# Second norm's scaling and power chain on GpSimd, small statistics first, urgent value and norm products allowed into dense work

## The chip, the cores and the metric

The kernel runs on one core of one Trainium2 chip. The metric is the device time in microseconds (us), as the median of several executions; a lower time is better. Beside the timed executions, each kernel has one profiled execution, whose trace gives what each engine did and when. The span of a profiled execution, from the first to the last instruction, is up to five us off the timed median. Engines in the trace: PE is TensorE's products (PEld its weight loads), DVE is VectorE, ACT is ScalarE, POOL is GpSimd, SP issues transfers.

## The reference, cut to what matters

Two pairs of layers on a sequence of 2048 tokens of width 512. Each A layer is attention with 32 heads that share one key and one value head of width 16; each B layer is two norms, a mixing MLP with shifted channels and an MLP of width 1792. Cut:

```python
def _A_ref(x, wq, wk, wv, wo):
    q = ...                                   # 32 heads of width 16
    k, v = x @ wk, x @ wv                     # one head, shared
    p = softmax(einsum("bhqd,bkd->bhqk", q, k) * 16 ** -0.5)
    return einsum("bhqk,bkd->bhqd", p, v)... @ wo

def _B_ref(x, w1, w2, w3, w4):
    h = gelu(layernorm(x) @ w1)               # then four channel groups shifted by 1, -1, 2, -2
    x1 = x + hs                               # hs = shifted @ w2
    return x1 + gelu(layernorm(x1) @ w3) @ w4

x = x + A(layernorm(x)); x = x + B(layernorm(x))      # layer 1
x = x + A(layernorm(x)); x = x + B(layernorm(x))      # layer 2
```

Note that B norms a row that was normed just before it: B receives layernorm(x), and norms that again. The kernel computes the second factor from the first variance by a chain of small operations, and this is the "second norm" of the title.

## The kernel before

The kernel is a Python program that plans before it emits. It declares operations with their reads, writes and an assumed duration, lets a planner place them on the five engines in simulated time, and then writes each engine's instructions in the planned order. On the chip each engine runs its list in that order and waits on semaphores. So the order is fixed, but the times are not: an instruction whose inputs come late holds up everything behind it in its engine's list.

Attention in one unit: TensorE makes scores (QK), ScalarE takes the exponential of 128x1024 of them into one of seven EA buffers, TensorE multiplies them by V (the "value product", accumulating in one PSUM bank). Some units are given to VectorE and GpSimd instead, as a "pair": VectorE turns scores into integers J (two instructions of 128x512), GpSimd, or VectorE if GpSimd is behind, adds constants (two instructions JK), and the bits read as bf16 are near the exponential. Dense work (projections and MLPs) and norms fill the gaps. When nothing is ready, TensorE multiplies zeros by ones ("filler"). This is meant to keep its clock up; a4 below shows a stretch in which it did not.

The parts that the change and the argument touch:

```python
# planner, choosing TensorE's next operation (cut)
stick = eng == "PE" and not dense and not joins and self.STICK is not None \
    and t < self.pe_end + 0.05 and self.pe_kind == "P"
...
key = (low.get(o, o.prio), o.seq)                 # smaller goes first; scores have 0, value products 2
...
if stick and o.prio > 2 and o.pe[0] == self.pe_kind and not any(... for x in due):
    key = (self.STICK, o.seq)                     # -1: a run of dense products is kept together

# when a pair may be declared (cut)
def attach(self, q):
    if sum(1 for t, b in self.pl.pool if t + 0.06 <= self.pl.now) >= self.FREE:   # FREE = 2 of 3 banks
        self.assign(self.pl.now, 1 - q.pe[3][0] // 2)     # also: pairs under way, VectorE's backlog

# rstd: the power -1/2 of the variance (and of the second norm's variance), cut
op("DVE", ... tensor_scalar(out=var, in0=mv, scalar1=EPS, op0=add))
if both:
    op("DVE", ... reciprocal(aux, var)); op("DVE", ... aux * mv); op("DVE", ... aux + EPS)
op("POOL", ... tensor_tensor(out=SM[:, 0:k], in0=SM[:, 2:2 + k], in1=MH, op=pow))   # one call for both

# mixer_in: the second norm's scaling
op("DVE", ... tensor_scalar(out=ZR[:, tb % 4], in0=Y[:, tb % 6], scalar1=SM[:, 1, tb], op0=mult), dur=0.265)

# ln_in: the next layer's normed rows also go to ZR
self.apply(self.ZR[:, tb % 4, :], src(tb), tb, ...)

URGE = ((10, 10, 10, 1.0), (10, 10, 10, 1.5, 10))     # base priority of what follows each chunk
```

The softmax here doesn't subtract the row's maximum and nothing guards it: scores larger than these inputs give would overflow.

## Time and profile before

| | before |
|---|---|
| timed median | 1616.96 us (1616.88 to 1617.77, 3 runs) |
| span of the profiled execution | 1615.1 us |
| exponentials on ScalarE | 1504, 1390.6 us |
| pairs on VectorE and GpSimd | 544 (1088 J instructions / 2) |
| fillers on TensorE | 1984 |
| end of the last exponential | 1549.26 us |

The lines are in the prediction below. The way to read them is to ask, for each stretch, which engine has no idle time: ScalarE in the two long attention stretches, none at the change of layers (760 to 935 us), TensorE and chains of waits in the tail after the last exponential.

Up to the end of its last exponential, ScalarE's time is the exponentials, the idle time ahead of them (66.6 us by the page), and the rest (Gelu, table loads, their waits): 1549.26 = 1390.6 + 66.6 + 92.1. After it comes the tail, 1615.1 - 1549.26 = 65.8 us.

### The profile page before, as it was taken

The page shows a single profiled execution, that of the slowest core. Times are in us where ns is not written, and L with a number is a line of the kernel's source. Part 1 is how long each engine was busy: PE and PEld are TensorE (multiplying, and loading weights), DVE is VectorE, ACT ScalarE, POOL GpSimd, SP SyncE. Part 2 cuts the span into 40 slices and gives each one's busy share as a digit, 9 for nine tenths or more (in the row PEclk, how much of TensorE's full clock was granted, in tenths as well). Part 3 has the DMA queues.
Part 4 walks back from the last instruction along what each step waited for, and adds up shares of the span by engine and source line. Part 5 has one row for each costly group of instructions (what it writes and reads, how often), then busy time and mean ns, then how long its engine had stood idle before and what let it go on. Part 6 is the DMA issues. An engine that isn't in the chain of part 4 may idle for free.

```text
span 1615.1 us, 63788 instructions
## 1 busy us (share of the span) xinstructions
PE 1567.6 (97%) x28953; PEld 654.9 (41%) x28953; DVE 1245.5 (77%) x2222; ACT 1500.5 (93%) x1580; POOL 1118.4 (69%) x1083
## 2 busy tenths in 40 slices
PE   8999999999999999999999999999999999999999
PEld 3333333434333333333333434333343334544555
DVE  8777887778887679887776678878678885778863
ACT  4999999999999999999998499999999998999952
POOL 4798877866787766776673477677777867768631
PEclk9999999999999999999999999999999999999999
DMA  6100010001000001000000000100000000000000
GB/s 207 17 6 5 7 18 6 6 4 17 7 6 4 6 4 19 6 4 2 2 2 2 3 9 9 19 4 5 9 18 5 6 5 15 16 8 7 6 17 19
DMA packets 32144, 21.55 MB, mean 13 GB/s; under 512 B 12672, under 2 KB 31360, under 8 KB 31872
## 3 DMA queue, kind: packets, MB, share of 16 engines
q1 hardware_dynamic: 31872, 17.47, 4.5%
q8 instruction: 226, 3.70, 1.0%
q14 instruction: 46, 0.38, 0.1%
HBM read 7.90 MB, written 2.10 MB: 6 GB/s over the span
## 4 chain that ended last, share of the span: by engine, by line
ACT 64%; PE 33%; DVE 2%; issue 0%; DMA 0%; POOL 0%; SPq 0%; POOLq 0%
ACT EA L994 59%; PE PB L612 12%; PE PB L950 10%; PE PB L1073 8%; ACT G L1403 2%; PE PB L769 1%; ACT L994 1%; ACT GP L1323 1%; ACT L1403 1%; ACT L1323 0%; DVE ZR L752 0%; DVE ST L723 0%; DMA X<-in_A_x_dram 0%; DVE J L1015 0%; PE PB L878 0%
## 5 line engine op out<-in xcount | busy, mean ns | idle before, releaser
L994 ACT ACTIVATE EA<-PB 128x1024 bf16<-128x1024 f32 x1504 | 1390.6, 1105 | 66.6 <-PE PB L1073 33.8
L1025 POOL TENSOR_SCALAR JK<-J 128x1024 uint16<-128x1024 uint16 x983 | 1035.6, 1054 | 402.4 <-DVE J L1015 257.4
L1015 DVE TENSOR_SCALAR J<-PB 128x512 uint16<-128x512 f32 x1088 | 702.4, 683 | 185.1 <-PE PB L950 181.1
L950 PE MATMUL PB<-QT,KT 32*128 32x512 bf16 (+1 forms) x4608 | 624.4, 359 | 30.5 <-ACT EA L994 18.6
L1073 PE MATMUL PB<-EA,VP 128*32 128x256 bf16 (+1 forms) x6784 | 388.4, 265 | 0.5
L950 PEld LDWEIGHTS PB<-QT,KT 32*128 32x128 bf16 x4608 | 161.3, 91 | 448.0 <-ACT EA L994 351.4
L1073 PE MATMUL PB<-JK,VD 128*32 128x256 bf16 (+1 forms) x4864 | 291.3, 265 | 2.9 <-POOL JK L1025 1.9
L1073 PEld LDWEIGHTS PB<-EA,VP 128*32 128x32 bf16 x6784 | 157.1, 95 | 175.3 <-issue 149.6
L612 PE MATMUL PB<-ONES,NIL 128*32 128x512 bf16 x1984 | 177.1, 387 | 7.4 <-DVE ZR L752 2.8
L1073 PEld LDWEIGHTS PB<-JK,VD 128*32 128x32 bf16 x4864 | 114.9, 95 | 128.0 <-issue 78.8
L612 PE MATMUL PB<-ZT,W 128*32 128x512 bf16 (+2 forms) x2816 | 166.6, 341 | 0.0
L1073 PE MATMUL PB<-J,VD 128*32 128x256 bf16 (+1 forms) x2432 | 154.9, 264 | 1.3 <-DVE J L1015 0.8
L612 PE MATMUL PB<-W,G 128*32 128x512 bf16 x1792 | 122.9, 380 | 0.3 <-DVE X L1279 0.3
L1396 DVE CAST G<-PB 128x512 bf16<-128x512 f32 (+2 forms) x126 | 72.3, 582 | 34.7 <-PE PB L612 33.4
L612 PEld LDWEIGHTS PB<-ZT,W 128*32 128x32 bf16 x2816 | 67.7, 96 | 26.1 <-issue 13.0
L1025 DVE TENSOR_SCALAR JK<-J 128x1024 uint16<-128x1024 uint16 x105 | 73.2, 702 | 2.9 <-PE PB L1073 1.9
L1073 PEld LDWEIGHTS PB<-J,VD 128*32 128x32 bf16 x2432 | 60.6, 95 | 35.4 <-issue 21.6
L612 PEld LDWEIGHTS PB<-ONES,NIL 128*32 128x32 bf16 x1984 | 49.6, 96 | 42.4 <-issue 11.2
L745 POOL TENSOR_TENSOR SM<-SM,MH 128x4 f32<-128x4 f32 (+4 forms) x30 | 31.7, 1058 | 40.8 <-DVE SM L737 24.8
L1133 DVE TENSOR_TENSOR OS<-ACCF,PB 128x512 bf16<-128x512 bf16 (+1 forms) x72 | 44.6, 622 | 17.7 <-PE PB L1127 17.3
L612 PEld LDWEIGHTS PB<-W,G 128*32 128x32 bf16 x1792 | 42.2, 96 | 31.8 <-issue 11.7
L1403 ACT ACTIVATE G<-G 128x3584 bf16<-128x3584 bf16 (+2 forms) x18 | 46.0, 2601 | 9.4 <-DVE G L1396 9.3
(88 smaller groups left out, 861.5 us busy)
## 6 DMA issues: line engine op xcount, KB each, us to landing
OT<-OS SPq DMA_DIRECT2D x424, 8.0 KB, 1.8
W<-in_B_w_dram SPq DMA_DIRECT2D x2, 1792.0 KB, 14.4
QT<-QS SPq DMA_DIRECT2D x40, 64.0 KB, 2.4
X<-in_A_x_dram SPq DMA_DIRECT2D x8, 256.0 KB, 5.4
out_dram<-OUTB SPq DMA_DIRECT2D x16, 128.0 KB, 1.7
OT<-OS SPq DMA_DIRECT2D x104, 4.0 KB, 1.7
W<-in_B_w_dram SPq DMA_DIRECT2D x2, 512.0 KB, 8.4
WQ<-in_A_wq_dram SPq DMA_DIRECT2D x1, 512.0 KB, 5.0
```

Of the source, the lines that this page charges most:

```text
L612: ins = e.matmul(self.PB[32 * g:32 * g + 32, bank, 0:n], lhsT=lhsT[:, 32 * g:32 * g + 32], rhs=rhs, start=start, stop=stop, tile_position= ...
L745: op("POOL", lambda e: e.tensor_tensor(out=self.SM[:, 0:k, a:b], in0=self.SM[:, 2:2 + k, a:b], in1=self.MH[:, 0:k, a:b], op=ALU.pow), read ...
L769: ins = e.transpose(self.PBH[:, L.bank, j * 512 + i * 128:j * 512 + (i + 1) * 128], self.ZR[:, tb % 4, dc * 128:(dc + 1) * 128], self.IDENT)
L950: ins = e.matmul(self.PB[:, bank, j * n:(j + 1) * n], lhsT=self.KT[32 * h:32 * h + 32, la, (kb + j) * 128:(kb + j + 1) * 128], rhs=self.QT ...
L994: o = q.feeds = op("ACT", lambda e: e.activation(self.EA[:, ea, :, :], self.PB[:, b0:b0 + 2, :], ACTF.Exp, scale=0.25), writes=bk + [("EA" ...
L1015: o = op("DVE", lambda e, i=i, L=L: e.tensor_scalar(out=J[:, i * 512:(i + 1) * 512], in0=self.PB[:, L.bank, :], scalar1=128 * LOG2E * 0.25 ...
L1025: x = op(eng, lambda e, k=k, r=r: e.tensor_scalar(out=self.JK[:, r, :], in0=J, scalar1=float(self.STEPS[k]), scalar2=1.0, op0=ALU.add, op1 ...
L1073: ins = e.matmul(self.PB[32 * x:32 * x + 32, self.ACC, p * hw:p * hw + hw], lhsT=v[:, la, kb + j, :], rhs=ap[:, i, j * w + u * hw:j * w + ...
L1133: op("DVE", lambda e: e.tensor_tensor(out=self.OS[:, m, 0:n], in0=acc, in1=self.PB[:, M.bank, 0:n], op=ALU.mult), reads=[("ACCF", m)], wri ...
L1323: return e.activation(self.GP[:, par, :, 2:2 + n], self.GP[:, par, :, 2:2 + n], ACTF.Gelu_apprx_tanh)
L1396: op("DVE", lambda e, f=f, L=L: e.tensor_copy(self.G2[:, f, 0:n], self.PB[:, L.bank, 0:n]), writes=[L, ("G2", f)], dur=t_ps(n), give=L)
L1403: ins = e.activation(self.G2[:, a:a + 7, 0:n], self.G2[:, a:a + 7, 0:n], ACTF.Gelu_apprx_tanh)
```

## The change

It takes 32 scalings and the small norm instructions off VectorE, and changes the planner's rules. The intent: VectorE is relieved for pairs; small statistics go first; value products that ScalarE is about to wait for are "pinned" ahead of dense work; urgent norm work breaks a run of dense products; the last chunk's work gets a high priority and a buffer of its own; the next layer's normed rows get the buffer QS, so that they need not wait for ZR. Cut to its core:

```diff
+    PINNED = -2
+    RUSHED = 1.2
@@ planner
         stick = ... and self.pe_kind == "P" \
+            and not any((0 < o.prio <= self.RUSHED if o.side else self.closing) and o.ready <= t + 1e-9 for o in h)
+        pinned = {p for u in self.units[-3:] if not u.placed for p in u.preds
+                  if p.eng == "PE" and p.prio == 2 and not p.placed} if eng == "PE" and not dense else ()
+            if eng == "ACT" and self.closing and o.side and not all(u.placed for u in self.units[-4:]):
+                continue
+            if o in pinned:
+                key = (self.PINNED, o.seq)
@@ kernel
-    URGE = ((10, 10, 10, 1.0), (10, 10, 10, 1.5, 10))
+    URGE = ((10, 10, 10, 1.0), (10, 10, 10, 1.5, 1.0))
+    RUSH = ((10, 10, 10, 1.0), (10, 10, 10, 5, 1.0))     # priority of a block's norm products, 5 before
@@ rstd: a power call for each norm, the small instructions on POOL (not in the head)
-            op("DVE", ... reciprocal(aux, var)) ...
+            op(eng, ... tensor_tensor(out=aux, in0=one, in1=one, op=mult)) ...
@@ ln_in
+        base = (self.QS, "QS") if la else (self.ZR, "ZR")
@@ mixer_in
-            op("DVE", lambda e, tb=tb: e.tensor_scalar(
+            op("POOL", lambda e, tb=tb: e.tensor_scalar(
...
-               dur=0.265, port=True)
+               dur=0.71, prio=self.QUICK, port=True)
@@ last MLP: Gelu output in the EA buffers
-                op("ACT", lambda e, f=f, L=L: e.activation(self.G2[:, f, 0:n], ...
+                op("ACT", lambda e, f=f, L=L: e.activation(self.G2E[:, f, 0:n], ...
```

## The prediction

> **What bounds the kernel now.** I read the page first, then the busy time of the engines in four stretches that I chose from the 40 slices, then what ScalarE waits for, then ScalarE and TensorE in order of time at its gaps. All figures below are of the one profiled execution of the kernel before (span 1615.1 us; the timed median is 1616.96 us).
>
> The page's engine row and its three costliest rows; columns of a row: line, engine, operation, output and input, count, then busy us and mean ns, then idle time before it:
>
> ```profile
> PE 1567.6 (97%) x28953; PEld 654.9 (41%) x28953; DVE 1245.5 (77%) x2222; ACT 1500.5 (93%) x1580; POOL 1118.4 (69%) x1083
> ...
> L994 ACT ACTIVATE EA<-PB 128x1024 bf16<-128x1024 f32 x1504 | 1390.6, 1105 | 66.6 <-PE PB L1073 33.8
> L1025 POOL TENSOR_SCALAR JK<-J 128x1024 uint16<-128x1024 uint16 x983 | 1035.6, 1054 | 402.4 <-DVE J L1015 257.4
> L1015 DVE TENSOR_SCALAR J<-PB 128x512 uint16<-128x512 f32 x1088 | 702.4, 683 | 185.1 <-PE PB L950 181.1
> ...
> L612 PE MATMUL PB<-ONES,NIL 128*32 128x512 bf16 x1984 | 177.1, 387 | 7.4 <-DVE ZR L752 2.8
> ```
>
> PE's 97% is not a bound everywhere: the last row is products of zeros that only keep TensorE busy. Four side by side are one step of 512 columns; 112 equal products in the tail take 6.05 us, so a step is 6.05/28 = 0.216 us and the 1984/4 = 496 filler steps are 107 us of room. The exponentials are done in two ways: 1504 on ScalarE (1390.6/1504 = 0.925 us each), and 1088/2 = 544 "pairs" by a bit trick on VectorE and GpSimd.
>
> The stretches (columns: PE, PEld, DVE, ACT, POOL busy us and count, granted clock, DMA share, GB/s):
>
> ```profile
> 40.00:760.00 720.00, 701.63 (x11972) 276.17 (x11964) 579.52 (x979) 718.39 (x760) 552.90 (x528) 1.00 0.04 8
> 760.00:935.00 175.00, 168.64 (x2864) 69.35 (x2866) 124.12 (x242) 142.37 (x145) 90.20 (x88) 1.00 0.01 2
> 935.00:1550.00 615.00, 602.00 (x12341) 260.11 (x12338) 481.24 (x852) 603.12 (x637) 452.66 (x435) 1.00 0.04 9
> 1550.00:1615.10 65.10, 60.25 (x1288) 34.17 (x1286) 25.99 (x62) 18.51 (x23) 5.53 (x6) 1.00 0.06 21
> ```
>
> In the first and third ScalarE is full (718 of 720, 603 of 615): there only fewer exponentials on ScalarE, or no gaps, shorten the time. The second is the change of layers: 175 - 142.4 = 32.6 us of ScalarE are lost. The fourth is the tail, 65 us with no exponential, bound by TensorE and by chains.
>
> ScalarE's gaps in order of time (start, length, what, and in brackets the idle time before it and who ended it):
>
> ```profile
> 879.15 9.27 ACT L994 ACTIVATE EA<-PB 128x1024 bf16<-128x1024 f32 x10
> 898.57 1.02 ACT L994 ACTIVATE EA<-PB 128x1024 bf16<-128x1024 f32 x1 [10.15 <-PE PB L1073]
> ...
> 930.66 34.94 ACT L994 ACTIVATE EA<-PB 128x1024 bf16<-128x1024 f32 x38 [8.38 <-PE PB L950]
> ...
> 1181.93 18.44 ACT L994 ACTIVATE EA<-PB 128x1024 bf16<-128x1024 f32 x20 [3.11 <-PE PB L1073]
> ...
> 1369.39 1.94 ACT L994 ACTIVATE EA<-PB 128x1024 bf16<-128x1024 f32 x2 [5.19 <-PE PB L1073]
> ```
>
> The releaser L1073 is a value product (exponentials times V). The exponentials rotate through seven EA buffers; ScalarE stops when the product that reads the oldest has not run. TensorE was busy with dense work instead:
>
> ```profile
> 1365.16 3.19 PE L612 MATMUL PB<-W,G 128*32 128x512 bf16 x56
> 1368.18 1.05 PE L612 MATMUL PB<-YT,WQ 128*32 128x256 bf16 x32
> 1369.05 0.40 PE L1073 MATMUL PB<-EA,VP 128*32 128x128 bf16 x16
> ```
>
> **What the Trainium skill says.** "GPSIMD Engine Reference", section Engine selection, calls one-input elementwise work on GpSimd roughly line-rate and two-input work about twice as slow. The trace agrees on the first: 1024 elements in a median of 1044 ns; on two inputs, X<-Y,X takes 1169 ns for 512, about double per element. "Advanced Engine Details and Errata", VectorE Performance Modes, Mode Summary, says that GpSimd and VectorE's two-port modes block each other at a shared port. The trace fits: the scaling ZR<-Y,SM of VectorE takes 256 ns at best and 1134 at worst, and the add of epsilon on four numbers 149 to 1028, the excess being about one GpSimd add. "Perfetto Trace Analysis", Identifying the Most-Contended Engine, warns that matmul busy share is no measure of headroom; here the fillers are why.
>
> **The change, part by part.**
>
> 1. VectorE to GpSimd. Off VectorE go 32 scalings ZR<-Y,SM (16.8 us busy), the reciprocal, product and add of the two-norm groups (1.5 + 3.9 + 3.8), and 26 of the 30 epsilon adds (9.5 x 26/30 = 8.2): 34.2 us. GpSimd gets 32 x about 0.6 (half of a 1024-element add plus the reading of a scalar: 19 us), 26 + 27 small ones at about 0.2 (as its 8-element copies, 191 to 219 ns: 10.6 us) and power as two calls of 4 numbers, 2 x 1.015 against 1.641 for 8 (0.4 x 7 groups: 2.7 us): about 32 us on an engine that idles 497. VectorE spends 702.4/544 = 1.29 us per pair plus 73.2/544 = 0.13 for the adds that fall back on it, 1.43. So at most 34.2/1.43 = 24 more pairs, each worth 0.925 us of ScalarE: 22 us. A pair is declared only while two PSUM banks are free and few pairs are under way, and VectorE already idles 185 us waiting for score products, so I take a third: 8 pairs, **-8 us**. TensorE pays for a pair 3.5 steps (two score steps, three half steps of values) against 1.5: 2 x 0.216 = 0.43 us, 3.5 us for 8, from 81 us of fillers in these stretches.
>
> 2. Value products pinned ahead of dense work. In the full stretches the waits of this kind sum to 9.5 us (0.2 + 3.1 at 1176-1182, 5.2 + 0.4 + 0.4 + 0.2 at 1364-1382). Nearly all should go: **-8 us**. At the change of layers some 20 us of such waits go too, but there it is no gain by itself: ScalarE runs out of scores whose keys exist (the 8.38 us wait for L950 at 930), and the keys come when TensorE has done the dense chain. Fed without gaps, ScalarE reaches that wait earlier and waits longer. Only a shorter chain (transposes and norm products no longer behind a run of dense products; QS in place of ZR for the next layer's rows) helps: **-2 us**.
>
> 3. The tail. From the output projection at 1553.88 to the last product at 1612.1 are 58.2 us. The dense products in it, counted in steps: 8 (WO) + 126 (W,G) + 36 (288 of 256 columns) + 12 (W,GP) + 42 (224 of 384) = 224 x 0.216 = 48.4 us. So 9.8 us are chain waits, fillers and transposes:
>
> ```profile
> 1580.67 0.67 PE L612 MATMUL PB<-ONES,NIL 128*32 128x512 bf16 x8
> 1581.54 1.02 PE L612 MATMUL PB<-ONES,NIL 128*32 128x512 bf16 x12 [0.20 <-DVE ST L723]
> 1582.75 1.26 PE L612 MATMUL PB<-ONES,NIL 128*32 128x512 bf16 x20 [0.18 <-DVE MV L725]
> 1584.66 0.40 PE L612 MATMUL PB<-ONES,NIL 128*32 128x512 bf16 x4 [0.65 <-DVE ZR L752]
> ```
>
> The last chunk's work now has priority 1.0 instead of 10, and its Gelu output goes into the free EA buffers, so it need not wait until older chunks' products have read G2. Its two norm chains then lie beside 24 us of older chunks' dense work (12 W,G, 6 of W3, 6 W,G). The waits of 1580.67-1587.3 (6.6 us less 0.8 of transposes) should be filled; the 1.8 us after the projection stay, since the Gelu of 1550.57-1556.84 still comes after the last exponential: **-6 us**. The longer power chain on GpSimd costs nothing there: scaling now ends at 1562.2; with 0.2 + 0.7 + 3 x 0.2 + 0.7 + 2 x 0.6 us after the statistics at 1558.1, plus hand-overs, it ends at much the same time.
>
> Sum: -8 - 8 - 2 - 6 = -24 us. The whole order of instructions is planned anew, and slots won in one place are partly lost in another; I keep nine tenths: -22 us, 1595 us.
>
> **Rivals.**
> - GpSimd becomes the wait. Scalings stand in its queue among 1.04 us adds and lengthen each norm chain by 2 to 3 us, and more adds fall back on VectorE (105 now). For it: the chains matter at the change of layers. Against: 31% idle, and a wait of at most 8.4 us for its inputs, not for itself. Alone it would take back the pairs' 8 us and add some 3: about 1606.
> - TensorE becomes the bound: removed gaps in ScalarE merely displace dense work, as at the change of layers, and the tail inherits it. For it: the stretch 1360-1400 has only 1.39 us of fillers. Against: 60 us of fillers in the third stretch as a whole. Then only the tail and a few pairs remain: about 1606.
> - VectorE's backlog was what held pairs back. For it: it is 80% busy in the first stretch, and the worst shared-port cases vanish with it. All 24 pairs would give -22 instead of -8, and the waits at the change of layers might shrink by 5 more: about 1577.
>
> **Range and chances.** The first two rivals put the upper side at about 1606 and a poor replanning at 1611; the third, taken half, puts the lower side at 1580. 2% below is 1584.6: it needs the third rival nearly whole, chance 0.15. Slower by 2% would need a broken chain; each part moves work to an engine with room: 0.01.
>
> **What would show it.** Fewer ScalarE exponentials and as many more J rows (8 halves: 1496 and 1104); the total of ScalarE waiting for L1073 from 33.8 us to under 10; a wait for L950 at the change of layers longer than 8.4 us; no filler group in the tail after the projection longer than 2 us; VectorE's rows for ZR<-Y,SM gone and about 0.6 us each on GpSimd. It would be wrong if the number of pairs fell, if the stretch between the layers shortened or lengthened by over 6 us, or if GpSimd's scaling took over 1 us.

## The result, and the profile after

The changed kernel took 1598.39 us (median of 4 runs, 1597.78 to 1599.63) against 1616.97 us of the kernel before on the same chip (1616.88 to 1617.77). The ratio is 0.9883 with a 95% interval of 0.9869 to 0.9897. Ratios are the mean time of one kernel's fast runs over that of the other's fast runs of the same rounds, so they are not quite the ratio of the medians quoted. The prediction was 1595 us with a range of 1580 to 1611.

The page of the changed kernel, engine row and the rows that answer to those of before (line, engine, operation, output and input, count, then busy us and mean ns, then idle before):

```profile
PE 1553.5 (97%) x28709; PEld 648.2 (41%) x28709; DVE 1214.7 (76%) x2145; ACT 1506.4 (94%) x1585; POOL 1133.5 (71%) x1149
...
L1017 ACT ACTIVATE EA<-PB 128x1024 bf16<-128x1024 f32 x1509 | 1397.6, 1088 | 47.1 <-PE PB L973 37.6
...
L1038 DVE TENSOR_SCALAR J<-PB 128x512 uint16<-128x512 f32 x1078 | 698.9, 683 | 195.1 <-PE PB L973 190.9
...
L625 PE MATMUL PB<-ONES,NIL 128*32 128x512 bf16 x1764 | 153.8, 388 | 6.6 <-DVE ZR L773 1.7
```

VectorE is busy 30.8 us less than before. But the relief bought no pairs: there are 1078/2 = 539, five fewer, and ScalarE has five exponentials more. What fell is ScalarE's idle time ahead of exponentials, from 66.6 to 47.1 us, and the number of fillers.

The same sum as before: the last exponential ends at 1536.75 us = 1397.6 + 47.1 + 92.05, and the tail is 1597.5 - 1536.75 = 60.75 us. So the span's 17.6 us less are:

| term | before | after | difference |
|---|---|---|---|
| exponentials on ScalarE | 1390.6 | 1397.6 | +7.0 |
| idle time ahead of them | 66.6 | 47.1 | -19.5 |
| rest of ScalarE up to there | 92.1 | 92.05 | 0 |
| tail | 65.8 | 60.75 | -5.1 |

Where the idle time went shows in ScalarE's timeline of the changed kernel (start, length, what; in brackets the idle time before it and who ended it):

```profile
871.64 16.85 ACT L1017 ACTIVATE EA<-PB 128x1024 bf16<-128x1024 f32 x18
894.73 12.26 ACT L1017 ACTIVATE EA<-PB 128x1024 bf16<-128x1024 f32 x13 [6.24 <-PE PB L1096]
...
927.62 124.49 ACT L1017 ACTIVATE EA<-PB 128x1024 bf16<-128x1024 f32 x135 [14.73 <-PE PB L973]
```

L1096 is the value product's line now, L973 that of the scores. At the change of layers the long wait for a value product is 6.2 us and not 10.2, and the wait for the scores of the last keys grew from 8.4 to 14.7 us, as ScalarE arrives there earlier; the scores come 3.0 us earlier than before (927.62 against 930.66). After it the kernel before had gaps of 11.0 us in sum (10.5 of them for value products, 0.5 for scores); the changed kernel shows none that the timeline lists.

TensorE in the tail, in order of time:

```profile
1550.63 1.48 PE L625 MATMUL PB<-W,G 128*32 128x512 bf16 x24
1551.94 1.92 PE L625 MATMUL PB<-ZT,W 128*32 128x256 bf16 x64
1553.68 1.47 PE L625 MATMUL PB<-W,G 128*32 128x512 bf16 x24
1554.98 2.76 PE L625 MATMUL PB<-W,GP 128*32 128x512 bf16 x48
1557.57 4.92 PE L625 MATMUL PB<-W,G 128*32 128x512 bf16 x88
```

The last chunk's products (ZT,W and W,GP) now lie inside the older chunk's W,G. In the kernel before, 224 of those ran ahead of them, 112 before the last chunk's transposes (IDENT,ZR) and 112 after:

```profile
1563.62 0.62 PE L769 MATMUL PB<-IDENT,ZR 128*128 128x128 bf16 x8
1564.17 6.23 PE L612 MATMUL PB<-W,G 128*32 128x512 bf16 x112
1570.22 3.01 PE L612 MATMUL PB<-ZT,W 128*32 128x256 bf16 x104
```

The fillers for the last norm, which took some five us in the kernel before, are one group of 0.79 us.

The operations that moved, on GpSimd:

```profile
L1314 POOL TENSOR_SCALAR ZR<-Y,SM 128x512 bf16<-128x512 bf16 x32 | 22.2, 711 | 0.9
...
L758 POOL TENSOR_SCALAR SM<-MV 128x4 f32<-128x4 f32 x12 | 2.8, 233 | 19.5 <-DVE MV L738 18.7
```

### The profile page after: what moved, and what is told of

The parts are those of the page before. It is cut to its first block, busy times and chain, and to the rows that moved or that the text cites. A ratio compares the mean times of both kernels' runs of the same rounds, so it can differ in the third digit from the quotient of the medians.

```text
span 1597.5 us, 63318 instructions
## 1 busy us (share of the span) xinstructions
PE 1553.5 (97%) x28709; PEld 648.2 (41%) x28709; DVE 1214.7 (76%) x2145; ACT 1506.4 (94%) x1585; POOL 1133.5 (71%) x1149
## 4 chain that ended last, share of the span: by engine, by line
ACT 73%; PE 24%; DVE 3%; DMA 0%; issue 0%; POOL 0%; SPq 0%; POOLq 0%
ACT EA L1017 68%; PE PB L625 9%; PE PB L973 7%; PE PB L1096 6%; ACT G L1428 2%; ACT L1017 1%; PE PB L791 1%; ACT GP L1348 1%; ACT L1428 1%; DVE ST L736 0%; ACT L1348 0%; DVE G L1421 0%; DMA X<-in_A_x_dram 0%; DVE J L1038 0%; PE PB L901 0%
## 5 line engine op out<-in xcount | busy, mean ns | idle before, releaser
L1017 ACT ACTIVATE EA<-PB 128x1024 bf16<-128x1024 f32 x1509 | 1397.6, 1088 | 47.1 <-PE PB L973 37.6
L1048 POOL TENSOR_SCALAR JK<-J 128x1024 uint16<-128x1024 uint16 x955 | 1009.3, 1057 | 354.6 <-DVE J L1038 229.6
L973 PE MATMUL PB<-QT,KT 32*128 32x512 bf16 (+1 forms) x4608 | 623.8, 360 | 26.0 <-ACT EA L1017 15.0
L1096 PE MATMUL PB<-EA,VP 128*32 128x256 bf16 (+1 forms) x6796 | 385.3, 264 | 0.9 <-DVE QT L1108 0.5
L973 PEld LDWEIGHTS PB<-QT,KT 32*128 32x128 bf16 x4608 | 160.5, 91 | 434.8 <-ACT EA L1017 312.9
L1096 PE MATMUL PB<-JK,VD 128*32 128x256 bf16 (+1 forms) x4840 | 288.7, 265 | 2.9 <-POOL JK L1048 1.9
L1096 PEld LDWEIGHTS PB<-EA,VP 128*32 128x32 bf16 x6796 | 159.0, 95 | 159.1 <-issue 128.7
L625 PE MATMUL PB<-ZT,W 128*32 128x512 bf16 (+2 forms) x2816 | 170.4, 342 | 0.2
L1096 PEld LDWEIGHTS PB<-JK,VD 128*32 128x32 bf16 x4840 | 114.3, 95 | 135.3 <-issue 83.3
L625 PE MATMUL PB<-ONES,NIL 128*32 128x512 bf16 x1764 | 153.8, 388 | 6.6 <-DVE ZR L773 1.7
L1096 PE MATMUL PB<-J,VD 128*32 128x256 bf16 (+1 forms) x2420 | 153.3, 263 | 1.4 <-DVE J L1038 0.6
L625 PE MATMUL PB<-W,G 128*32 128x512 bf16 x1624 | 114.4, 383 | 1.1 <-ACT G L1428 1.1
L1048 DVE TENSOR_SCALAR JK<-J 128x1024 uint16<-128x1024 uint16 x123 | 80.9, 664 | 4.9 <-PE PB L1096 3.6
L625 PEld LDWEIGHTS PB<-ZT,W 128*32 128x32 bf16 x2816 | 63.8, 96 | 32.4 <-issue 18.6
L1096 PEld LDWEIGHTS PB<-J,VD 128*32 128x32 bf16 x2420 | 59.8, 95 | 37.1 <-issue 22.7
L625 PEld LDWEIGHTS PB<-ONES,NIL 128*32 128x32 bf16 x1764 | 43.7, 96 | 42.1 <-issue 10.4
L1428 ACT ACTIVATE G<-G 128x3584 bf16<-128x3584 bf16 (+2 forms) x18 | 46.0, 2602 | 14.9 <-DVE G L1421 14.8
L1157 DVE TENSOR_TENSOR OS<-ACCF,PB 128x512 bf16<-128x512 bf16 (+1 forms) x72 | 44.8, 622 | 17.5 <-PE PB L1151 16.7
L756 POOL TENSOR_TENSOR SM<-SM,MH 128x4 f32<-128x4 f32 (+3 forms) x39 | 37.0, 950 | 22.3 <-DVE SM L758 19.4
L625 PEld LDWEIGHTS PB<-W,G 128*32 128x32 bf16 x1624 | 37.3, 96 | 29.7 <-issue 13.8
```

Of the source, the lines that this page charges most:

```text
L625: ins = e.matmul(self.PB[32 * g:32 * g + 32, bank, 0:n], lhsT=lhsT[:, 32 * g:32 * g + 32], rhs=rhs, start=start, stop=stop, tile_position= ...
L756: op("POOL", lambda e: e.tensor_tensor(out=out, in0=src, in1=self.MH[:, 0, a:b], op=ALU.pow), reads=tags + [("MH",)], writes=tg(r), dur=0. ...
L973: ins = e.matmul(self.PB[:, bank, j * n:(j + 1) * n], lhsT=self.KT[32 * h:32 * h + 32, la, (kb + j) * 128:(kb + j + 1) * 128], rhs=self.QT ...
L1017: o = q.feeds = op("ACT", lambda e: e.activation(self.EA[:, ea, :, :], self.PB[:, b0:b0 + 2, :], ACTF.Exp, scale=0.25), writes=bk + [("EA" ...
L1048: x = op(eng, lambda e, k=k, r=r: e.tensor_scalar(out=self.JK[:, r, :], in0=J, scalar1=float(self.STEPS[k]), scalar2=1.0, op0=ALU.add, op1 ...
L1096: ins = e.matmul(self.PB[32 * x:32 * x + 32, self.ACC, p * hw:p * hw + hw], lhsT=v[:, la, kb + j, :], rhs=ap[:, i, j * w + u * hw:j * w + ...
```

## The experiments

Twelve kernels ran, in three groups of four, each group on one chip with the kernel before. All gave a correct result. "Planned anew" means that the planner ran with the stated rules, so that every instruction may change place. "Held order" means that the plan of before or after was kept, and only the named instructions were moved. On the three chips the kernel before took 1616.99, 1617.56 and 1616.96 us (medians of seven runs each). Where a difference in us is taken between kernels of different groups, or to the 1616.97 us of before above, it can be off by the half microsecond by which these differ.

| run | kernel | median us | ratio to before, 95% interval |
|---|---|---|---|
| a1 | after, norm work to VectorE, held order | 1617.15 | 0.9979 to 1.0026 |
| a2 | before, norm work to GpSimd, held order | 1620.82 | 1.0010 to 1.0040 |
| a3 | before, late value products ahead, held order | 1618.62 | 0.9991 to 1.0021 |
| a4 | before, tail rules only | 1616.64 | 0.9977 to 1.0010 |
| b1 | before with the pin only, planned anew | 1627.51 | 1.0050 to 1.0080 |
| b2 | after without the pin, planned anew | 1643.65 | 1.0146 to 1.0176 |
| b3 | before, a neutral constant changed | 1625.35 | 1.0033 to 1.0063 |
| b4 | after, norm work on VectorE, planned anew | 1604.07 | 0.9902 to 0.9936 |
| c1 | before with pin and QS, planned anew | 1613.14 | 0.9959 to 0.9992 |
| c2 | after, pairs at one free bank | 1592.07 | 0.9833 to 0.9872 |
| c3 | after, the same neutral constant changed | 1616.31 | 0.9978 to 1.0008 |
| c4 | after, six planner constants changed | 1581.67 | 0.9768 to 0.9797 |

The first theory, A, was that of the prediction put sharply: the order of TensorE's work made the gain, and the engine of the norm work did not. Its rivals are named in the expectations.

### a1: the norm work back on VectorE, order held

```diff
             self.pl.run(self.pump)
+            for o in self.scalings:          # 32 scalings, 53 small norm instructions
+                self.pl.order[o.eng].remove(o)
+                o.eng = "DVE"
+                self.pl.order[o.eng].append(o)
+            self.pl.renumber()               # sort each engine's list by planned start
```

> The changed kernel with every instruction in its planned place, only that the 32 scalings and the 53 small norm instructions go back from GpSimd to VectorE (the second power stays a second call). Theory A (the order of TensorE's work made the gain, the engine of the norm work did not): 1596 to 1603 us, same within 0.3%. Rival B (relief of VectorE and of the shared port made it): 1606 us or more, with VectorE's busy time up by some 30 us and waits of ScalarE back.

Measured: 1617.15 us (1614.12 to 1622.19), the whole gain gone, and inside the range of rival B. The waits of ScalarE, first the changed kernel, then a1 (total us, times, longest):

```profile
ACT EA L1017 <- PE PB L973: 37.6, 11, 18.3
```

```profile
ACT EA L1031 <- PE PB L987: 47.5, 33, 18.4
```

There are 22 more short waits for scores, most of 0.2 to 0.7 us. The waits for value products stayed at 8.8 us, and the tail too (1612.2 - 1551.42 = 60.8 us). So theory A failed as stated: in this order the engine does matter. The likely reason is that VectorE's list had no room planned for these instructions; the extra hand-overs between VectorE and GpSimd in the power chain are another, which a1 doesn't separate. In the profile of a1 the granted clock also dips to 0.91 in three 20-us slices and not in one (540 to 560, which the changed kernel has as well), and ScalarE's gaps at 1414 to 1426 and 423 to 440 lie in the two others, about 3 us each. Whether the dips made these gaps or the gaps the dips is not known. They do not carry the whole loss: the two runs with a mean granted clock of 0.996 (0.998 to 0.999 in the changed kernel) still took 1614 us.

### a2: the norm work to GpSimd in the order of before

```diff
+            for o in self.scalings:          # 32 scalings, 26 epsilon adds
+                ... o.eng = "POOL" ...
```

> The kernel before with every instruction in its planned place, only that the 32 scalings and 26 epsilon adds run on GpSimd. Theory A: 1613 to 1620 us, no gain, and the gaps of ScalarE before the value products stay (33.8 us in total). Rival B: 1609 us or less.

Measured: 1620.82 us, just above what A expected, and clearly not rival B. VectorE's busy time fell from 1245.5 to 1226.6 us, the waits for value products stayed at 33.8 us, and nothing was gained. a1 and a2 together show a one-sided thing: in these fixed orders, work put on an engine cost at once, while work taken off it gave nothing back by itself, as the other instructions stay in their places.

### a3: late value products moved ahead, order held

```diff
+            for u in self.units:
+                for p in u.preds:
+                    if p.eng == "PE" and p.prio == 2:        # a value product
+                        t = (when its inputs were planned to be there)
+                        if p.start > t + 4.0:
+                            p.start = t + 4.0
+            self.pl.renumber()
```

> The kernel before, with the 63 value products that were planned over 4 us after their inputs moved forward to 4 us after them; nothing else changes place. Theory A: ScalarE's waits for value products after the change of layers fall from 10.3 us to under 3 and the time falls by 7 to 11 us, to 1606 to 1610; at the change of layers the waits for value products go too, but the wait for scores grows from 8.4 us to some 20, so nothing is gained there. Rival C (TensorE is the bound, and gaps only displace dense work): 1614 us or more.

Measured: 1618.62 us, no gain; rival C's time. In ScalarE's timeline of a3, at the place where before waited 5.19 us for a value product:

```profile
1366.83 1.94 ACT L1010 ACTIVATE EA<-PB 128x1024 bf16<-128x1024 f32 x2 [3.02 <-PE PB L1089]
1371.29 4.91 ACT L1010 ACTIVATE EA<-PB 128x1024 bf16<-128x1024 f32 x5 [2.53 <-PE PB L966]
```

L1089 is the value product, L966 the scores. The wait was not removed but handed on: two exponentials start earlier, and the next one waits for scores that still stand behind the dense run, since in the plan they were placed for the late time. Over the whole run waits for value products fell from 33.8 to 8.8 us, waits for scores rose from 31.8 to 45.0 and those of Gelu for VectorE from 9.3 to 19.9. Moving one of two things that stand behind a dense run gained nothing here.

### a4: the tail rules alone

```diff
-    URGE = ((10, 10, 10, 1.0), (10, 10, 10, 1.5, 10))
+    URGE = ((10, 10, 10, 1.0), (10, 10, 10, 1.5, 1.0))
 (and the last Gelu's output in EA, as in the change)
```

> The kernel before with only the last chunk's priority 1.0 in place of 10 and its Gelu output in the EA buffers; up to the last exponential the order is that of before. Theory A: last exponential at the same time, the tail after it shorter by 4 to 6 us: 1611 to 1613. Rival D (the tail also needs the breaking of dense runs): under 2 us gained, 1615 or more.

Measured: 1616.64 us, rival D's time. Two things are in it. In the profiled execution the last exponential ended at 1552.26 us, 3.0 later than before, although the order up to there is the same. The view of 20-us stretches of a4 (busy time and count of GpSimd, granted clock, DMA share, GB/s) has the reason:

```profile
880.00:900.00 20.00, 4.39 (x5) 0.83 0.01 2
```

Before had 1.00 there. This is a lapse of TensorE's clock, in which eight filler-sized products took 1.04 us in place of 0.61. The order of work there is that of before, so no moved instruction explains it. The tail itself became 1614.8 - 1552.26 = 62.5 us, 3.3 less than before and 1.8 more than after. Its timeline:

```profile
1566.50 0.62 PE L782 MATMUL PB<-IDENT,ZR 128*128 128x128 bf16 x8
1567.05 6.23 PE L624 MATMUL PB<-W,G 128*32 128x512 bf16 x112
1573.10 3.01 PE L624 MATMUL PB<-ZT,W 128*32 128x256 bf16 x104
```

The transposes broke in, but the last chunk's first products (ZT,W) still waited for 112 products of an older chunk, which the stick rule kept together. In the changed kernel they stand between 24 and 24. So the priority and the buffer are worth about 3 of the tail's 5 us in the profile. The breaking of the runs is the likely source of the rest, but it was not tested alone.

The median of the timed runs shows no gain, but each run lists its mean granted clock. Three of a4's four runs have a mean granted clock of 0.997, the profiled one among them, and took 1616.55 to 1616.88 us. The fourth has 0.999 and took 1614.65. The kernel before had 0.998 or 0.999 in all seven runs on this chip, and those with 0.999 average 1616.97. So at an equal clock the tail rules gain about 2.3 us, by one run. Why a4 had the lower clock in three runs of four stays open.

### b1 and b2: the pin alone, and everything but the pin

After the first four runs I formed theory E: the parts work through one joint plan, and the pin pays only together with others. Both kernels are planned anew.

```diff
 # b1: before, plus
+        pinned = {...}
+            if o in pinned:
+                key = (self.PINNED, o.seq)
 # b2: after, with
-                  if p.eng == "PE" and p.prio == 2 and not p.placed} if eng == "PE" and not dense else ()
+        pinned = ()
```

> The kernel before, planned anew with the pinned value products only. After the four runs with held order, the revised theory E: the gain is in the joint order, the pin takes away the waits after the keys of layer 2 but alone it makes those keys later. E: waits of ScalarE for value products after the keys under 2 us (before 10.3), the wait for the first scores of layer 2's last keys longer than 8.4 us and later than 930.7 us by 20 us or more, the time no better: 1617 to 1632. The prediction's step (pin worth 8 us by itself): 1606 to 1611.

> The changed kernel, planned anew without the pinned value products. E: most of the gain is lost or turned into a loss, since all the other parts move work of other kinds ahead of value products: 1620 to 1645, with waits of ScalarE for value products after the keys over 25 us in total. If the pin only displaced work (rival C): 1598 to 1606.

Measured: b1 1627.51 us, 10 us slower than before; b2 1643.65 us, 45 us slower than after. The lines of ScalarE, b1's timeline first, then b2's waits:

```profile
938.96 137.51 ACT L1008 ACTIVATE EA<-PB 128x1024 bf16<-128x1024 f32 x149 [13.06 <-PE PB L964]
```

```profile
ACT EA L1017 <- PE PB L1096: 62.1, 30, 7.6
```

In b1 the waits for value products after 945 us fell from 10.5 to 2.6 us (I had expected under 2), so the pin does what it is meant to. But the scores of the last keys came at 938.96 us, 8.3 us later than before (I had expected 20 or more), and ScalarE waited 13.06 us for them. Just before stands a wait that the kernel before did not have:

```profile
919.36 3.28 ACT L1419 ACTIVATE G<-G 128x1792 bf16<-128x1792 bf16 x2 [11.17 <-DVE G L1412]
```

By the sum used above, b1's idle time ahead of exponentials is 55.0 us, 11.6 less than before. The exponentials take 4.3 us more (1507 of them), and the rest and the tail together 17.4 us more, of which this wait before a Gelu is 11.2. So the pin shortened the waits that it aims at, and the time was lost at the change of layers. That the pin alone gains 8 us did not come out; but b1 is one plan, and b3 below shows that 10 us between two plans can be luck. b2 shows the other side: with all the other parts and no pin, ScalarE waits 62.1 us for value products, 36.0 of them after 945 us. These 45 us are more than twice the largest difference that b3 and c3 below put down to luck, so among the other parts of the change the pin is needed.

### b3 and c3: how much a plan is worth by luck

```diff
-    MARGIN = 0.15
+    MARGIN = 0.151          # b3 in before, c3 in after
```

The constant is a margin in the planner's arithmetic. It has no meaning for the work, it only decides which of nearly equal choices is taken, and from the first different choice on the order differs (and with it a few pairs: 542 in both b3 and c3, where before has 544 and after 539).

> The kernel before, with one constant of its planner (the margin that it adds before an instruction of TensorE) at 0.151 instead of 0.150 us, which changes no work, only the order that is planned. It measures how much a new plan is worth by luck. E: differs from before by 5 us or more, probably slower (1622 to 1635), since before was the best of its neighbours. Rival F (the plan is robust): within 2 us of 1617.

> The changed kernel with the margin constant 0.151 in place of 0.150, the counterpart of b3. E: the changed kernel was a lucky plan as well: 1608 to 1620, so that the change is worth some 10 to 17 us with this constant too (b3 is 1625.4). Rival F (the plan of the changed kernel is robust): within 3 us of 1598.4.

Measured: b3 1625.35 us, 8.4 us slower than before; c3 1616.31 us, 17.9 us slower than after. Both expectations held, rival F fell in both. In c3 the waits for value products are 26.0 us (8.8 in after), in b3 40.4 us (33.8 in before). With this constant the same change is worth 1625.35 - 1616.31 = 9.0 us and not 18.6. ScalarE's exponentials, b3 first, then c3:

```profile
L994 ACT ACTIVATE EA<-PB 128x1024 bf16<-128x1024 f32 x1506 | 1393.4, 1102 | 73.8 <-PE PB L1073 40.4
```

```profile
L1017 ACT ACTIVATE EA<-PB 128x1024 bf16<-128x1024 f32 x1506 | 1396.3, 1089 | 63.3 <-PE PB L973 36.0
```

The same sum for both constants tells what the two comparisons have in common. The rest and the tail are taken together, since in b3 one Gelu more stands ahead of the last exponential.

| what the change does to | constant 0.150 (before, after) | constant 0.151 (b3, c3) |
|---|---|---|
| exponentials on ScalarE | +7.0 | +2.9 |
| idle time ahead of them | -19.5 | -10.5 |
| rest of ScalarE and tail | -5.1 | -1.5 |
| span | -17.6 | -9.1 |

In both, most of the gain is idle time ahead of exponentials, and no attention pair is won. The waits for value products after the keys went from 10.5 us to none with one constant and from 17.1 to 8.3 with the other. Two constants are no distribution, but they show that a difference of 10 us, and up to 18, between two plans of this kernel may be luck of the plan. Of b1, b4, c1 and c2 the time alone therefore proves little.

### b4: the norm work on VectorE, planned anew

```diff
 (rstd and the scaling as in before; all the other parts of the change kept)
```

> The changed kernel with the scaling and the power chain back on VectorE as before, planned anew. E: a good part of the gain stays, 1602 to 1613 (the loss of a1 came from VectorE's order having no room for them). Rival B (the engine of the norm work made the gain): 1615 or more.

Measured: 1604.07 us, so 12.9 of the 18.6 us remain without the move to GpSimd (1616.97 - 1604.07). The 5.7 us between b4 and after are less than the luck that b3 and c3 show, so what the move is worth by itself stays open. That it is not the main part is likely, but 12.9 us is within that luck too. That a1's loss was that of an order with no room, and not of the engine, fits b4; one plan doesn't show it.

### c1: the pin with the QS buffer

```diff
 # before, with the pin (as b1) and
+        base = (self.QS, "QS") if la else (self.ZR, "ZR")
```

> The kernel before with two parts of the change, planned anew: the pinned value products, and the next layer's normed rows in QS in place of ZR. E (the pin needs the shorter key chain): against b1 the first scores of the last keys of layer 2 come at least 30 us earlier than 939 us and the time is 8 to 14 us less than b1's 1627.5: 1613 to 1620. If the QS buffer is a detail: within 4 us of b1.

Measured: 1613.14 us, 14.4 us less than b1 (8 to 14 expected) and 3.8 less than before; the time is inside the range. Keys of layer 2 are copied out of PSUM by VectorE; the last two such copies are one tile's keys (128x128), the first that the early units lack, and the last four tiles' (128x512). b1 first, then c1:

```profile
920.35 0.29 DVE L832 CAST KT<-PB 128x128 bf16<-128x128 f32 x1 [0.51 <-PE PB L825]
937.78 0.69 DVE L832 CAST KT<-PB 128x512 bf16<-128x512 f32 x1 [1.16 <-PE PB L825]
```

```profile
865.66 0.28 DVE L832 CAST KT<-PB 128x128 bf16<-128x128 f32 x1
920.98 0.69 DVE L832 CAST KT<-PB 128x512 bf16<-128x512 f32 x1 [1.35 <-PE PB L825]
```

The first of these keys come 54.7 us earlier, the last ones 16.8. My expectation of 30 us named 939 us, so it meant the last keys, and failed. ScalarE's wait before the last keys' scores is 2.51 us in c1, 13.06 in b1. In the kernel before these keys came at 903.82 and 929.49 us, in the changed one at 889.41 and 926.44. This is consistent with the code: in ZR the next layer's rows wait until the MLP's rows of the same slots have been transposed, in QS they need not. The trace shows the earlier keys; that the ZR slot was what they waited for is read from the code.

Two things limit what c1 says. By the sum, 6.5 us of the 14.4 are idle time ahead of exponentials and 10.4 the rest and the tail (the exponentials take 2.5 more); the 11.2 us before a Gelu just ahead of the keys are gone. And c1 has the pin, but its waits for value products after the keys are 10.5 us, as in the kernel before; one of them is 9.15. So the pin does not remove these waits in every plan, and that QS is what makes it pay is consistent with c1, not shown.

### c2: what limits the pairs

```diff
-    FREE = 2
+    FREE = 1
```

> The changed kernel with a pair declared when one PSUM bank is free instead of two. G (banks, not VectorE's time, hold the pairs back): over 10 pairs more than the 539 of the changed kernel, ScalarE's exponentials down by as many, 1585 to 1597. Rival H (VectorE's time holds them back): at most 3 pairs more, or more pairs and no time gained: 1596 or more.

Measured: 1592.07 us (1591.84 to 1597.99), 6.3 us less than after's median. The exponentials of ScalarE in c2:

```profile
L1017 ACT ACTIVATE EA<-PB 128x1024 bf16<-128x1024 f32 x1493 | 1383.9, 1070 | 45.3 <-PE PB L973 26.4
```

That is 16 fewer than after, so 555 pairs and not 539. The adds that fall back on VectorE rose from 123 to 234, and VectorE's busy share from 76% to 82%: it had the time in the changed kernel too. So the condition on free PSUM banks held pairs back; theory G stands, and H falls as it was stated. The margin is small: plans with two free banks had 539 to 549 pairs (549 in b2), and the difference in time is below the luck of a plan.

### c4: a version that beats both

```diff
-    SWITCH = 0.097
+    SWITCH = 0.095
-    BUNCH = 2
+    BUNCH = 4
-    PATIENCE = 3.0
+    PATIENCE = 4
-    ADDS = 4
+    ADDS = 5
-    FREE = 2
+    FREE = 1
-    LONELY = 3
+    LONELY = 2
```

> The changed kernel with six constants of its planner changed together (a pair at one free bank, lonely 2, bunch 4, patience 4, adds 5, switch 0.095), chosen by planning many settings without a chip: 568 pairs, 1480 exponentials on ScalarE. E and G: faster than both kernels, 1566 to 1578. If more pairs load TensorE past its fillers (rival C): 1590 or more.

If plans differ by luck, one can choose among many. The planner needs no chip, so many settings were planned and the shortest plan was built. Measured: 1581.67 us (1580.94 to 1584.58), ratio 0.9783 to before, 35.3 us less than before and 16.7 less than after; 4 us above the expected range.

```profile
L1017 ACT ACTIVATE EA<-PB 128x1024 bf16<-128x1024 f32 x1480 | 1376.4, 1060 | 38.0 <-PE PB L973 26.2
...
L625 PE MATMUL PB<-ONES,NIL 128*32 128x512 bf16 x1392 | 120.9, 394 | 6.7 <-DVE ZR L773 2.0
```

ScalarE has 29 exponentials fewer than in after (21.2 us) and 9.1 us less idle time ahead of them, and TensorE 372 fillers fewer. Part of that is given back in ScalarE's waits for VectorE before a Gelu, 28.8 us against 14.8. Which of the six constants did it was not tested; with 568 pairs, the 21.2 us of exponentials are work saved, not only a luckier order.

## Why the prediction was right or wrong

The total was right: 1595 predicted, 1598.4 measured, inside the range and on the right side of 2%. Its parts were not all right, and two of the errors partly cancelled: the exponentials took 7.0 us more where about 8 less were predicted, and the idle time ahead of them fell by 19.5 us where about 10 were. After b3 and c3, that the sum came so near is in part luck.

**Part 1, pairs, -8 us: wrong in sign.** The failed step is "I take a third: 8 pairs". There were five pairs fewer, and exponentials on ScalarE took 7.0 us more. The prediction itself named a condition that mattered, two free PSUM banks, and then counted a third of the freed time all the same; c2 shows that this condition held pairs back. Why there are fewer is open: with the other constant (b3, c3) there are 542 in both, so the five may be luck of the plan. That the relief won none holds in both. The costs themselves were nearly right: VectorE's busy time fell by 30.8 us (34.2 predicted), most small instructions took 0.23 to 0.27 us on GpSimd (0.2), the scaling 0.711 (0.6).

**Part 2, the pin, -8 us after the change of layers: the effect was there, the reason only half.** The gaps after the keys went from 11.0 us to none (the prediction's list of 9.5 us left out one of 1.07 at 1314). But the prediction counted this as a gain of the pin alone, and in b1's plan the pin alone lost 10 us: the gaps after the keys nearly went, but the last keys of layer 2 came later, and a wait before a Gelu stood ahead of them. That it would be no gain at the change of layers was foreseen, with the longer wait for scores (14.7 us against 8.4); that it could be a loss there was not. "Nearly all should go" held in this plan; with the other constant 8.3 us of 17.1 stayed (c3 against b3), a fall of 8.8 us.

**Change of layers, -2 us: about right in what counts, under-sized in what lies beneath.** The scores of the last keys came 3.0 us earlier (0.9 with the other constant: 930.45 in c3, 931.33 in b3). ScalarE's idle time in 760 to 935 us fell from 32.6 to 175 - 153.4 = 21.6, of which most was spent on four exponentials more before the keys and on gaps of about 2.8 us early in the run, which the kernel before did not have. The part that the prediction mentioned in half a sentence, QS in place of ZR, may be what makes the pin pay (c1 against b1), though the 14.4 us between these two plans are within luck.

**Part 3, the tail, -6 us: right in this plan, 5.1 measured.** The fillers before the last norm went, the fillers after the output projection stayed, as said. In a4 the priority and the buffer alone gave 3.3 of it. With the other constant, rest and tail together fell by only 1.5 us.

**The discount, nine tenths: far too little.** The prediction says that the order is planned anew and keeps nine tenths for that. b3 and c3 show that a plan changed for no reason moves the time by 8 and 18 us. That is the size of the whole effect. The range of 31 us was right for this reason more than for the rivals it was derived from.

**The rivals.** GpSimd did not become the wait: the profile names no engine that waited for a scaling, and GpSimd itself waited 229.6 us for J before its adds. (The prediction's "at most 8.4 us" for its inputs holds for these adds only; the kernel before had one wait of 12.6 us before a small copy.) TensorE as the bound (C) was right in a way that I had not meant: in a held order (a3) a gap removed at one product reappears at the next. Against VectorE's backlog as the limit of pairs speaks c2.

**The signs.** ScalarE's waits for value products fell below 10 us (8.8), the wait for scores grew, and the scalings left VectorE and took about 0.7 us on GpSimd: three signs as foretold. The sign about fillers in the tail, none over 2 us, tells nothing: the longest after the projection was 1.68 us in the kernel before. Fewer exponentials, the first sign, failed, and "the number of pairs fell" was on the list of what would make the prediction wrong: the mechanism was wrong there, though the total was not.

What stays open is how the 18.6 us split between rules and luck. With one neutral constant they are 18.6, with another 9.0. Shown are that the idle time ahead of exponentials falls in both, and that without the pin the change loses; the shares of QS, of the move to GpSimd and of the tail rules are not.

## What to carry to other kernels

Time freed on an engine is a gain only if that time is what held other work back; look for the condition that admits the other work (here, among others, two free PSUM banks) before counting the freed time. Where a planner fixes the order, change a constant that means nothing, in both kernels, before believing a difference of a per cent, and use the same spread to choose a better plan. A wait that names one product may hide a second one behind the same run: look whether both can move before counting it.

## What the Trainium skill lacked or had wrong

- "TensorE: Matmul & The Clock Gate", HAM oscillation, gives the abstract rule that no idle gap of TensorE should exceed about 3.4 us. In a4 the granted clock was 0.83 in 880 to 900 us, after a stretch with fillers in which the longest idle gap that the timeline lists is 1.72 us; the kernel before, in the same order and with the same gap, kept 1.00. So shorter gaps were no guarantee here. The page promises none, and what set the lapse off stays open.
- "GPSIMD Engine Reference", Engine selection, calls one-input work roughly line-rate. The scaling of 512 bf16 elements by one value for each partition took 711 ns on GpSimd; on VectorE, in the kernel before, it took 256 ns at best and 539 on average. So the statement holds to 1.3 times against the average, and is off by 2.8 times against the best.
- No page gives the cost of a power on GpSimd. The changed kernel shows means of 579 ns for one number in each partition, 765 for two, 882 for three and 1067 for four, the kernel before 1641 for eight.
- No page speaks of an order planned in advance. Here a constant changed by 0.001 us moved the time by 8.4 us in one kernel and by 17.9 in the other.
